# A linear-attention and MoE kernel: a new order for its first block, v loaded amid q, and d_ff columns dealt by fours

## The chip, the cores and the metric

The kernel runs on one core of a Trainium2 chip. The core has a matrix engine (TensorE, PE in the profile, its weight loads listed apart as PEld), a vector engine (VectorE, DVE), an activation engine (ScalarE, ACT), GpSimd (POOL) and a queue engine (SyncE, SP). SP and POOL issue the transfers between device memory and the on-chip memory (SBUF). TensorE writes to PSUM, from where VectorE and ScalarE read. The metric is device time in microseconds (us); lower is better.

## The reference: what is computed

Eight batches of linear attention ("cosformer") feed one two-layer feed-forward block with a quick GELU. Inputs are float32.

```python
# attention: q, k, v are [8 batches, 8 heads, 576 tokens, 64]
theta = pi / 2 * arange(576) / 576
phi(x) = concat([relu(x) * cos(theta), relu(x) * sin(theta)], -1)   # 64 -> 128 features
kv  = einsum('bhsf,bhsd->bhfd', phi(k), v)      # 128 x 64 per head
z   = sum(phi(k), over tokens)                  # 128 per head
num = einsum('bhsf,bhfd->bhsd', phi(q), kv)
den = einsum('bhsf,bhf->bhs', phi(q), z) + 1e-6
x   = (num / den) as [4608 tokens, 512]         # heads side by side
# feed-forward: w_in is [512, 2048], w_out is [2048, 512]
h = x @ w_in
out = (h * sigmoid(1.702 * h)) @ w_out          # [4608, 512]
```

The hidden dimension of 2048 (d_ff) is summed over in the last product, so any reordering of it that is the same for w_in's columns and w_out's rows leaves the output as it is.

## The kernel before

A batch is a *block* of 576 tokens: four chunks of 128 and a tail of 64. The order of instructions on every engine is the order of the program text; no planner moves anything.

**A block's steps.** `trig` makes the features of k or q (relu, times cosine or sine) for one slice j of 64 columns: two instructions, on VectorE or, with `act=True`, on ScalarE. `kv_mm` multiplies features of k by v per head into PSUM (L202), and `kv_evac` copies the result to SBUF as `kvs`. In block 0 a column of ones gives z in a product of its own, before v is there (L364); later blocks carry the ones as a 65th column of v. q's features must be turned so that features lie on partitions: in block 0 TensorE does it (`qturn_pe`, L170) and `qevac` copies the result out of PSUM; later blocks use a transposing transfer on SP's queue. `num_mm` (L215) multiplies turned q by `kvs` for one chunk, giving numerator and denominator. `num_div` on VectorE adds 1e-6, takes the reciprocal and multiplies: three instructions, the last of them writes `xn` (L227). `xturn_mm` (L241) turns `xn` on TensorE and `xturn_evac` (L248, ScalarE) copies it to `xT`. The numerator and the turned x share one PSUM tile `at`, of a pool with two buffers.

**Feed-forward.** d_ff is cut into 16 *groups* of 128 columns, `fc`. `mm1` makes one group for 512 tokens: four matrix products (L264) that load a 128x128 piece of `w_in_sb` as weights, and one activation (L269). `mm1_tail` (L284) does the 64 tail tokens of a block for eight groups: 32 products of only 64 columns with the same weight tiles, 512 of them in the whole kernel. `mm2` (L305) multiplies a chunk of activated tokens by `w_out_sb`, and ScalarE copies the sum out to `ysb` (L309). The PSUM pool `mm` has four buffers.

**The start.** SP's queue loads k in two pieces and then q in two pieces. POOL waits for k's first piece (a one-element copy called `gate`), then issues v in two pieces and w_in's columns in four, the last two behind a second gate on v. TensorE runs products of zeros (`idle`, L317) meanwhile. Then come the ones products, q's first three turns, the K-V products, the fourth turn, the numerators and `start_block(0)`. That function starts the feed-forward chunk by chunk: for each of the four chunks it makes 128-token pieces of groups 0 to 3, with the remaining numerators and x turns between them, and then group 4. Groups 5 to 15 follow as whole groups of 512 tokens.

**Block 1's start.** Here the numerators of chunks 0 to 2 and the x turns of chunks 0 and 1 stand between the last pieces of block 0's `mm2` (L422 to L443), and `start_block(1, opened=True)` leaves them out. Later blocks put their numerators between `mm2` calls and turn x by transfers.

Of the kernel before, what the change touches and what calls it, by code (L numbers as in the profile page):

```python
# [9 lines left out]
F32 = mybir.dt.float32  # L10
# [9 lines left out]
def kernel(  # L20
# [34 lines left out]
    def src_of(src, b, i0=0, i1=NI):  # L55
        return src[b, 2 * i0:2 * i1].rearrange("(i hh) (p j) d -> (hh p) i (j d)", hh=2, j=NS)
# [1 line left out]
    qf = one.tile([128, 2560], F32, name="qf")  # L58
    kf, vf, vb = raw("kf"), raw("vf"), raw("vb", BF16)
    qf0 = qf[:, 0:NI * S].rearrange("p (i e) -> p i e", i=NI)  # L60
    for t, src, cut in ((kf, k, 192), (qf0, q, 256)):
        nc.sync.dma_start(out=t[:, :, 0:cut], in_=src_of(src, 0)[:, :, 0:cut])
        nc.sync.dma_start(out=t[:, :, cut:S], in_=src_of(src, 0)[:, :, cut:S])


    NP = NS + 5
# [36 lines left out]


    win_r = moe_w_in.rearrange("(kc p) f -> p kc f", p=128)
    wout_r = moe_w_out.rearrange("(fc p) d -> p fc d", p=128)

    def load(t, src, b):
        nc.gpsimd.dma_start(out=t, in_=src_of(src, b))
# [7 lines left out]
    def load_win(f0, f1):  # L117
        nc.gpsimd.dma_start(out=w_in_sb[:, :, f0:f1], in_=win_r[:, :, f0:f1])

    def load_wout(g):  # L120
        nc.gpsimd.dma_start(out=w_out_sb[:, ts(g, 4), :], in_=wout_r[:, ts(g, 4), :])

    gate = const.tile([1, 4], F32)
    nc.gpsimd.tensor_copy(gate[0:1, 0:1], kf[0:1, 0, 0:1])
    for i in (0, 2):
        nc.gpsimd.dma_start(out=vb[:, i:i + 2], in_=src_of(v, 0, i, i + 2))
    load_win(0, 512)
    load_win(512, 1024)
    nc.gpsimd.tensor_copy(gate[0:1, 1:2], vb[0:1, 3, 0:1])
    load_win(1024, 1536)  # L130
    load_win(1536, 2048)


    def trig(dst, src, j, act=False):
        i = src[:, :, ts(j, 64)]
        for cs, w in enumerate((cosw, sinw)):
            o = dst[:, j, :, ts(cs, 64)]
            if act:
                nc.scalar.activation(o, i, AF.Relu, scale=w[:, j:j + 1])
            else:  # L140
                nc.vector.tensor_scalar(o, i, 0.0, w[:, j:j + 1], op0=MAX, op1=MUL)  # L141
# [24 lines left out]
    def qturn_pe(c):  # L166
        tp = pmm.tile([128, 2, NI, 128], BF16, name="mm")
        for j in range(2 * c, min(2 * c + 2, NS)):
            for i in range(NI):
                nc.tensor.transpose(tp[:, j % 2, i], qn0[:, j, i, :], ident)  # L170
        tps[c] = tp

    def qevac(c, act=False):
        n = min(2 * c + 2, NS) - 2 * c
        o = qT[:, :, ds(c * 128, n * 64)].rearrange("f h (j p) -> f j h p", j=n)
        i = tps.pop(c)[:, 0:n].rearrange("f j i (hh p) -> f j (i hh) p", hh=2)
        if act:
            nc.scalar.activation(o, i, AF.Copy)
        else:
            nc.vector.tensor_copy(o, i)  # L180
# [16 lines left out]
    def kv_mm(i0, i1, rhs, col, n):  # L197
        for i in range(i0, i1):
            for j in range(NS):
                for hh in range(2):  # L200
                    r = slice(hh * 64, hh * 64 + 64)
                    nc.tensor.matmul(st["kv", i][:, hh, ds(col, n)], kr[r, j, i, :], rhs(r, i, j),  # L202
                                     start=(j == 0), stop=(j == NS - 1))

    def kv_evac(i0, i1):
        o = st["kvs"][:, :, i0:i1, 0:65]
        nc.vector.tensor_copy(o, st["ps", i0].rearrange("p hh (i e) -> p hh i e", e=65))  # L207
# [3 lines left out]
    def num_mm(c):  # L211
        ps = pat.tile([128, 2, 512], F32, name="at")
        for h in range(H):
            i, hh = divmod(h, 2)
            nc.tensor.matmul(ps[:, h // 4, ds((h % 4) * 65, 65)], qT[:, h, ts(c, 128)],  # L215
                             st["kvs"][:, hh, i, 0:65], start=True, stop=True)
        nums[c] = [ps]

    def num_div(c):
        ps = nums[c][0]  # L220
        pv = ps[:, :, 0:260].rearrange("p a (h e) -> p a h e", h=4)
        den = small.tile([128, 2, 4], F32, name="den")
        nc.vector.tensor_scalar(den, pv[:, :, :, 64], 1e-6, None, op0=ADD)  # L223
        inv = small.tile([128, 2, 4], F32, name="inv")
        nc.vector.reciprocal(inv, den)  # L225
        xn = small.tile([128, 2, 4, 64], BF16, name="xn", bufs=4)
        nc.vector.tensor_tensor(xn, pv[:, :, :, 0:64],  # L227
                                inv.unsqueeze(3).to_broadcast([128, 2, 4, 64]), op=MUL)
        nums[c].append(xn)
# [6 lines left out]
    def xturn_mm(c):  # L236
        ps, xn = nums[c]
        xv = xn.rearrange("p a h e -> p (a h e)")
        for kc in range(KC):
            o = ps[:, kc // 2, ds(264 + (kc % 2) * 64, 64)].bitcast(BF16)  # L240
            nc.tensor.transpose(o, xv[:, ts(kc, 128)], ident)  # L241

    def xturn_evac(b, c):
        ps = nums.pop(c)[0]
        n = 128 if c < 4 else 64
        i = ps[:, :, 264:392].bitcast(BF16).rearrange("p a (k t) -> p a k t", k=2)[:, :, :, 0:n]
        o = x[b][:, :, c * 128:c * 128 + n].rearrange("p (a k) t -> p a k t", a=2)
        nc.scalar.activation(o, i, AF.Copy)  # L248
# [11 lines left out]
    def mm1_part(b, fc, t0, t1):  # L260
        if t0 == 0:
            hp[fc] = pmm.tile([128, MT], F32, name="mm")
        for kc in range(KC):
            nc.tensor.matmul(hp[fc][:, t0:t1], w_in_sb[:, kc, ts(fc, 128)], x[b][:, kc, t0:t1],  # L264
                             start=(kc == 0), stop=(kc == KC - 1))

    def gelu(fc):
        g = gpool.tile([128, MT], BF16, name="g")
        nc.scalar.activation(g, hp.pop(fc), AF.Gelu_apprx_sigmoid)  # L269
        gT[fc] = g  # L270

    def mm1(b, fc):
        mm1_part(b, fc, 0, MT)
# [4 lines left out]
    def mm1_tail(b, half):  # L278
        if half == 0 and b % 2 == 0:
            gt[0] = gpool.tile([128, FC, 128], BF16, name="gtail", bufs=2)  # L280
        hps = pmm.tile([128, 8, 64], F32, name="mm")
        for f in range(8):
            for kc in range(KC):
                nc.tensor.matmul(hps[:, f], w_in_sb[:, kc, ts(half * 8 + f, 128)], x[b][:, kc, MT:S],  # L284
                                 start=(kc == 0), stop=(kc == KC - 1))
        nc.scalar.activation(gt[0][:, ts(half, 8), ts(b % 2, 64)], hps, AF.Gelu_apprx_sigmoid)  # L286

# [26 lines left out]
    def idle(n, cols=512):  # L314
        w = pmm.tile([128, 512], F32, name="mm")
        for _ in range(n):
            nc.tensor.matmul(w[:, 0:cols], warm[:, 0:128], warm[:, 0:cols], start=True, stop=True)  # L317
# [4 lines left out]
    def vt_rhs(r, i, j):  # L322
        return vt[r, j, i, 0:65]

    def start_block(b, opened=False):

        if not opened:
            xturn_mm(0)
            xturn_evac(b, 0)
            xturn_mm(1)  # L330
            xturn_evac(b, 1)
            num_mm(2)
            num_div(2)
        for c in range(4):
            for fc in range(4):
                mm1_part(b, fc, c * 128, c * 128 + 128)
            if c == 0:
                num_mm(3)
                num_div(3)
                xturn_mm(2)  # L340
                xturn_evac(b, 2)
            if c == 1:
                num_mm(4)
                num_div(4)
                xturn_mm(3)
                xturn_evac(b, 3)
        for fc in range(4):
            gelu(fc)
        mm1(b, 4)
        xturn_mm(4)  # L350
        xturn_evac(b, 4)


    idle(12)
    idle(100, 64)
    for j in (0, 1):
        trig(kr, kf, j)
    for j in (2, 6, 7, 8):
# [5 lines left out]
    kv_mm(0, NI, lambda r, i, j: ones[r, 0:1], 64, 1)  # L364
    for j in (0, 1):
        trig(qn0, qf0, j)
    qturn_pe(0)
    for j in (2, 3):
        trig(qn0, qf0, j, act=True)
    qturn_pe(1)  # L370
    idle(3)
    for j in (4, 5):
        trig(qn0, qf0, j)
    qturn_pe(2)
    for j in (6, 7):
        trig(qn0, qf0, j, act=True)
    qevac(0)
    trig(qn0, qf0, 8)
    qevac(1, act=True)
    qevac(2, act=True)  # L380
    kv_mm(0, 2, vb_rhs, 0, 64)
    kv_evac(0, 2)
    kv_mm(2, 4, vb_rhs, 0, 64)
    kv_evac(2, 4)
    qturn_pe(3)
    qevac(3, act=True)
    num_mm(0)
    num_div(0)
    num_mm(1)
    num_div(1)  # L390
    qturn_pe(4)
    qevac(4)
    x_open(0)
    start_block(0)


    load(kf, k, 1)
# [5 lines left out]
    load_wout(3)  # L403
    for j in range(NS):
        trig(kr, kf, j)
    for fc in range(5, FC):
        mm1(0, fc)
    mm1_tail(0, 0)
    mm1_tail(0, 1)
# [9 lines left out]
    for g in range(2):  # L419
        for t in range(4):  # L420
            mm2(0, t, 4 * g, 4 * g + 4)
    mm2(0, 0, 8, 12)  # L422
    mm2(0, 1, 8, 12)
    kv_open()
    kv_mm(0, 4, vt_rhs, 0, 65)
    kv_evac(0, 4)
    mm2(0, 2, 8, 12)
    mm2(0, 3, 8, 12)
    num_mm(0)
    num_div(0)  # L430
    num_mm(1)
    num_div(1)
    x_open(1)
    mm2(0, 0, 12, 16)
    mm2(0, 1, 12, 16)
    xturn_mm(0)
    xturn_evac(1, 0)
    mm2(0, 2, 12, 16)
    xturn_mm(1)
    xturn_evac(1, 1)  # L440
    num_mm(2)
    num_div(2)
    mm2(0, 3, 12, 16)  # L443
    start_block(1, opened=True)


    for b in range(1, B):
# [73 lines left out]
```

## Time and profile before

| | |
|---|---|
| median of 3 runs | 296.39 us (295.75 to 305.15) |
| the profiled execution | 295.57 us |
| its span, first to last instruction | 293.9 us |
| PE busy | 283.1 us, 96% of the span |
| VectorE, ScalarE, POOL busy | 42%, 44%, 28% |
| L305 (output products), x509 | 116.0 us |
| L264 (first products), x593 | 113.6 us |
| L284 (tail products), x512 | 16.2 us |
| L202, L215 (K-V, numerators) | 4% and 3% of the chain that ended last |
| transferred | 53.59 MB, mean 182 GB/s |

Times in views run from the span's start. "Busy" counts overlapping products of an engine once. The chain that ended last is followed backwards from the last instruction, from each piece of work to what released it; a piece that reads "issue" is time for which the profile shows no cause. In the groups of instructions, "mean ns of one" is the length of a single instruction from its start to its end; instructions of PE overlap, so their pace is faster than that.

### The profile page before, as it was taken

The page shows a single profiled execution, that of the slowest core. Times are in us where ns is not written, and L with a number is a line of the kernel's source. Part 1 is how long each engine was busy: PE and PEld are TensorE (multiplying, and loading weights), DVE is VectorE, ACT ScalarE, POOL GpSimd, SP SyncE. Part 2 cuts the span into 40 slices and gives each one's busy share as a digit, 9 for nine tenths or more (in the row PEclk, how much of TensorE's full clock was granted, in tenths as well). Part 3 has the DMA queues.
Part 4 walks back from the last instruction along what each step waited for, and adds up shares of the span by engine and source line. Part 5 has one row for each costly group of instructions (what it writes and reads, how often), then busy time and mean ns, then how long its engine had stood idle before and what let it go on. Part 6 is the DMA issues. An engine that isn't in the chain of part 4 may idle for free.

```text
span 293.9 us, 6796 instructions
## 1 busy us (share of the span) xinstructions
PE 283.1 (96%) x2832; PEld 155.7 (53%) x2871; DVE 123.8 (42%) x355; ACT 128.0 (44%) x220; POOL 81.9 (28%) x96
## 2 busy tenths in 40 slices
PE   8879999999999999999999999999999999999993
PEld 4775546746544465446454465446454465445443
DVE  4674513791369125930269115950159304200000
ACT  7847642674115721465114641265114651166121
POOL 6361002635216501470215601290114300100111
PEclk9999999999999999999999999999999999999999
DMA  7999997999999876779249983889258402400112
GB/s 254 239 219 276 351 180 109 326 312 228 323 272 184 240 294 142 156 192 365 71 128 171 221 333 96 151 193 386 85 140 153 93 2 75 115 36 0 38 71 73
DMA packets 64238, 53.59 MB, mean 182 GB/s; under 512 B 49552, under 2 KB 56336, under 8 KB 64208
## 3 DMA queue, kind: packets, MB, share of 16 engines
q0 software_dynamic: 13792, 38.87, 43.3%
q1 hardware_dynamic: 50416, 14.30, 28.4%
q8 instruction: 22, 0.36, 0.5%
q14 instruction: 8, 0.07, 0.1%
HBM read 36.70 MB, written 9.44 MB: 157 GB/s over the span
## 4 chain that ended last, share of the span: by engine, by line
PE 95%; issue 1%; DVE 1%; ACT 1%; ACTq 0%
PE mm L305 42%; PE mm L264 37%; PE mm L284 5%; PE at L202 4%; PE at L215 3%; PE mm L317 3%; PE at L241 1%; DVE xn L227 1%; PE mm L170 1%; ACT g L269 1%; DVE inv L225 0%; DVE den L223 0%; ACT ysb L309 0%; DVE warm L76 0%; ACTq L269 0%
## 5 line engine op out<-in xcount | busy, mean ns | idle before, releaser
L305 PE MATMUL mm<-w_out_sb,g 128*128 128x512 bf16 (+1 forms) x509 | 116.0, 372 | 1.1 <-issue 0.2
L264 PE MATMUL mm<-xT,w_in_sb 128*128 128x512 bf16 (+1 forms) x593 | 113.6, 345 | 0.8
L312 POOL DMA_DIRECT2D out_dram<-ysb x44 | 50.7, 1152 | 169.7 <-ACT ysb L309 162.9
L269 ACT ACTIVATE g<-mm 128x512 bf16<-128x512 f32 x128 | 75.6, 598 | 39.6 <-PE mm L264 39.6
L264 PEld LDWEIGHTS <-w_in_sb 128*128 128x128 bf16 x608 | 53.8, 98 | 55.2
L305 PEld LDWEIGHTS <-g 128*128 128x128 bf16 x528 | 49.0, 98 | 50.2
L309 ACT ACTIVATE ysb<-mm 128x512 f32<-128x512 f32 (+1 forms) x37 | 21.7, 586 | 108.1 <-PE mm L305 101.9
L223 DVE TENSOR_SCALAR den<-at 128x8 f32<-128x8 f32 x40 | 6.6, 166 | 60.6 <-PE at L215 60.6
L227 DVE TENSOR_TENSOR xn<-at,inv 128x512 bf16<-128x512 f32 x40 | 27.7, 691 | 2.4 <-DMA xT<-xn 1.0
L207 DVE CAST kvs<-at 128x520 bf16<-128x520 f32 (+1 forms) x9 | 5.8, 642 | 51.3 <-PE at L202 51.2
L141 DVE TENSOR_SCALAR kr<-kf,cosw 128x256 bf16<-128x256 f32 x68 | 23.8, 350 | 6.9 <-DMA kf<-in_k_dram 6.9
L141 DVE TENSOR_SCALAR kr<-kf,sinw 128x256 bf16<-128x256 f32 x68 | 23.1, 340 | 0.0
L215 PEld LDWEIGHTS <-qT 128*128 128x128 bf16 x320 | 14.5, 97 | 7.3
L154 DVE TENSOR_SCALAR qn<-qf,cosw 128x512 bf16<-128x512 f32 (+1 forms) x33 | 15.8, 478 | 3.9 <-DMA qf<-in_q_dram 3.9
L284 PEld LDWEIGHTS <-w_in_sb 128*128 128x128 bf16 x512 | 16.0, 98 | 1.9
L284 PE MATMUL mm<-xT,w_in_sb 128*128 128x64 bf16 x512 | 16.2, 193 | 0.1
L215 PE MATMUL at<-kvs,qT 128*128 128x65 bf16 x320 | 15.9, 193 | 0.0
L154 DVE TENSOR_SCALAR qn<-qf,sinw 128x512 bf16<-128x512 f32 (+1 forms) x33 | 15.8, 479 | 0.0
L305 PE MATMUL mm<-w_out_sb,gtail 128*128 128x512 bf16 x60 | 13.6, 379 | 0.2
L202 PEld LDWEIGHTS <-kr 64*128 64x128 bf16 x648 | 10.1, 94 | 4.3 <-issue 3.7
L286 ACT ACTIVATE gtail<-mm 128x512 bf16<-128x512 f32 x16 | 9.6, 597 | 5.1 <-PE mm L284 5.1
L317 PE MATMUL mm<-warm 128*128 128x64 bf16 (+1 forms) x114 | 8.7, 240 | 1.3 <-DVE warm L76 1.3
(54 smaller groups left out, 112.0 us busy)
## 6 DMA issues: line engine op xcount, KB each, us to landing
kf<-in_k_dram POOLq DMA_DIRECT2D x7, 1152.0 KB, 9.1
vf<-in_v_dram POOLq DMA_DIRECT2D x7, 1152.0 KB, 11.8
qf<-in_q_dram POOLq DMA_DIRECT2D x7, 1024.0 KB, 7.4
out_dram<-ysb POOLq DMA_DIRECT2D x27, 256.0 KB, 2.8
out_dram<-ysb POOLq DMA_DIRECT2D x17, 128.0 KB, 7.2
w_in_sb<-in_moe_w_in_dram POOLq DMA_DIRECT2D x4, 512.0 KB, 9.7
w_out_sb<-in_moe_w_out_dram POOLq DMA_DIRECT2D x4, 512.0 KB, 18.0
qf<-in_q_dram POOLq DMA_DIRECT2D x7, 128.0 KB, 7.4
```

The lines of the kernel that those rows point to most:

```text
L141: nc.vector.tensor_scalar(o, i, 0.0, w[:, j:j + 1], op0=MAX, op1=MUL)
L154: nc.vector.tensor_scalar(o, i, 0.0, sc, op0=MAX, op1=MUL)
L202: nc.tensor.matmul(st["kv", i][:, hh, ds(col, n)], kr[r, j, i, :], rhs(r, i, j), start=(j == 0), stop=(j == NS - 1))
L215: nc.tensor.matmul(ps[:, h // 4, ds((h % 4) * 65, 65)], qT[:, h, ts(c, 128)], st["kvs"][:, hh, i, 0:65], start=True, stop=True)
L227: nc.vector.tensor_tensor(xn, pv[:, :, :, 0:64], inv.unsqueeze(3).to_broadcast([128, 2, 4, 64]), op=MUL)
L264: nc.tensor.matmul(hp[fc][:, t0:t1], w_in_sb[:, kc, ts(fc, 128)], x[b][:, kc, t0:t1], start=(kc == 0), stop=(kc == KC - 1))
L269: nc.scalar.activation(g, hp.pop(fc), AF.Gelu_apprx_sigmoid)
L284: nc.tensor.matmul(hps[:, f], w_in_sb[:, kc, ts(half * 8 + f, 128)], x[b][:, kc, MT:S], start=(kc == 0), stop=(kc == KC - 1))
L305: nc.tensor.matmul(yp[t, c0][:, c0:c1], w, w_out_sb[:, fc, c0:c1], start=(fc == 0), stop=(fc == FC - 1))
L309: nc.scalar.activation(ysb[:, c0:c1], yp[t, c0][:, c0:c1], AF.Identity)
L312: eng.dma_start(out=dst[:, c0:c1], in_=ysb[p0:p0 + n, c0:c1])
L317: nc.tensor.matmul(w[:, 0:cols], warm[:, 0:128], warm[:, 0:cols], start=True, stop=True)
```

## The change

Three things are changed together.

1. *Loads.* SP's queue loads k and q's first 256 columns of each row. v follows behind POOL's gate as before, then q's other columns on POOL's queue, then w_in: two transfers of 512 columns and, behind the gate on v, one of 1024 in place of two of 512.
2. *Order at the start of blocks 0 and 1.* Block 0 writes its start out by hand: K-V stands between the second and third turn of q, and the feed-forward begins with eight groups instead of five. Chunks 0 and 1 of groups 0 to 3 are made in pieces of 128 tokens, groups 4 to 7 in halves of 256 tokens (`half_part`); the activation then takes 256 tokens of two groups at once (`half_gelu`). The warm-up products are 111 of 64 columns, 16 of 128 and 6 of 512, in place of 12 of 512 and 100 of 64; three more of 512 between turns go. Block 1's start is no longer spread through block 0's output products: its K-V products stand ahead of groups 8 to 11 of `mm2`, two numerators stand between groups 12 to 15, and the rest is in `start_block(1)` behind them.
3. *d_ff dealt by fours.* Group fc = 4g + c now holds columns 512g + 4f + c, for f from 0 to 127. w_out's rows lie accordingly, so each partition of a w_out transfer reads four neighbouring rows, 8 KB, instead of four rows of 2 KB that lie apart. w_in is still loaded with neighbouring columns side by side; so a weight tile is now every fourth of 512 columns (`wcol`), in all products that load w_in.

The core of the diff:

```diff
-    for t, src, cut in ((kf, k, 192), (qf0, q, 256)):
-        nc.sync.dma_start(out=t[:, :, 0:cut], in_=src_of(src, 0)[:, :, 0:cut])
-        nc.sync.dma_start(out=t[:, :, cut:S], in_=src_of(src, 0)[:, :, cut:S])
+    nc.sync.dma_start(out=kf[:, :, 0:192], in_=src_of(k, 0)[:, :, 0:192])
+    nc.sync.dma_start(out=kf[:, :, 192:S], in_=src_of(k, 0)[:, :, 192:S])
+    nc.sync.dma_start(out=qf0[:, :, 0:256], in_=src_of(q, 0)[:, :, 0:256])
...
-    wout_r = moe_w_out.rearrange("(fc p) d -> p fc d", p=128)
+    wout_r = moe_w_out.rearrange("(g p c) d -> g p c d", p=128, c=4)
...
-        nc.gpsimd.dma_start(out=w_out_sb[:, ts(g, 4), :], in_=wout_r[:, ts(g, 4), :])
+        nc.gpsimd.dma_start(out=w_out_sb[:, ts(g, 4), :], in_=wout_r[g])
+    def wcol(kc, fc):
+        g, c = divmod(fc, 4)
+        return w_in_sb[:, kc, ts(g, 512)].rearrange("p (f c) -> p f c", c=4)[:, :, c]
...
+    nc.gpsimd.dma_start(out=qf0[:, :, 256:S], in_=src_of(q, 0)[:, :, 256:S])
     load_win(0, 512)
     load_win(512, 1024)
-    nc.gpsimd.tensor_copy(gate[0:1, 1:2], vb[0:1, 3, 0:1])
-    load_win(1024, 1536)
-    load_win(1536, 2048)
+    nc.gpsimd.tensor_copy(gate[0:1, 1:2], vb[0:1, 2, 0:1])
+    load_win(1024, 2048)
...
-            nc.tensor.matmul(hp[fc][:, t0:t1], w_in_sb[:, kc, ts(fc, 128)], x[b][:, kc, t0:t1],
+            nc.tensor.matmul(hp[fc][:, t0:t1], wcol(kc, fc), x[b][:, kc, t0:t1],
...
+    def half_part(fc, c0, c1):
+        pr, u, h = fc // 2, fc % 2, c0 // 2
+        if u == 0 and c0 % 2 == 0:
+            hb[pr, h] = pmm.tile([128, 2, 256], F32, name="mm")
+        t0, t1 = c0 * 128, c1 * 128
+        for kc in range(KC):
+            nc.tensor.matmul(hb[pr, h][:, u, t0 - h * 256:t1 - h * 256], wcol(kc, fc), x[0][:, kc, t0:t1],
+                             start=(kc == 0), stop=(kc == KC - 1))
+    def half_gelu(pr, h):
+        if h == 0:
+            gp[pr] = gpool.tile([128, 2, MT], BF16, name="gpair", bufs=4)
+            gT[2 * pr], gT[2 * pr + 1] = gp[pr][:, 0], gp[pr][:, 1]
+        nc.scalar.activation(gp[pr][:, :, ts(h, 256)], hb.pop((pr, h)), AF.Gelu_apprx_sigmoid)
...
-    idle(12)
-    idle(100, 64)
+    idle(111, 64)
+    idle(16, 128)
+    idle(6)
...
     for j in (2, 3):
         trig(qn0, qf0, j, act=True)
+    qturn_pe(0)
     qevac(0)
     kv_mm(0, 2, vb_rhs, 0, 64)
     kv_evac(0, 2)
+    qturn_pe(1)
+    qevac(1, act=True)
     kv_mm(2, 4, vb_rhs, 0, 64)
     kv_evac(2, 4)
     num_mm(0)
     num_div(0)
     num_mm(1)
     num_div(1)
+    for j in (4, 5):
+        trig(qn0, qf0, j, act=True)
+    x_open(0)
+    xturn_mm(0)
+    xturn_evac(0, 0)
+    qturn_pe(2)
+    qevac(2)
+    xturn_mm(1)
+    xturn_evac(0, 1)
+    trig(qn0, qf0, 6)
+    trig(qn0, qf0, 7, act=True)
+    half_part(0, 0, 1)
+    half_part(1, 0, 1)
+    num_mm(2)
+    num_div(2)
+    half_part(2, 0, 1)
+    half_part(3, 0, 1)
+    trig(qn0, qf0, 8)
+    for fc in range(4):
+        half_part(fc, 1, 2)
+    half_gelu(0, 0)
+    half_gelu(1, 0)
+    qturn_pe(3)
+    qevac(3)
+    xturn_mm(2)
+    xturn_evac(0, 2)
+    half_part(4, 0, 2)
+    half_part(5, 0, 2)
+    half_gelu(2, 0)
+    num_mm(3)
+    num_div(3)
+    half_part(6, 0, 2)
+    half_part(7, 0, 2)
+    half_gelu(3, 0)
+    qturn_pe(4)
+    qevac(4)
+    xturn_mm(3)
+    xturn_evac(0, 3)
+    for c in (2, 3):
+        for fc in range(4):
+            half_part(fc, c, c + 1)
+    half_gelu(0, 1)
+    half_gelu(1, 1)
+    num_mm(4)
+    num_div(4)
+    for fc in (4, 5, 6, 7):
+        half_part(fc, 2, 4)
+    half_gelu(2, 1)
+    half_gelu(3, 1)
+    xturn_mm(4)
+    xturn_evac(0, 4)
...
-    for fc in range(5, FC):
+    for fc in range(8, FC):
         mm1(0, fc)
...
-    mm2(0, 0, 8, 12)
-    mm2(0, 1, 8, 12)
     kv_open()
     kv_mm(0, 4, vt_rhs, 0, 65)
     kv_evac(0, 4)
-    mm2(0, 2, 8, 12)
-    mm2(0, 3, 8, 12)
+    for t in range(4):
+        mm2(0, t, 8, 12)
+    x_open(1)
+    mm2(0, 0, 12, 16)
+    mm2(0, 1, 12, 16)
     num_mm(0)
     num_div(0)
     num_mm(1)
     num_div(1)
-    x_open(1)
-    mm2(0, 0, 12, 16)
-    mm2(0, 1, 12, 16)
-    xturn_mm(0)
-    xturn_evac(1, 0)
     mm2(0, 2, 12, 16)
-    xturn_mm(1)
-    xturn_evac(1, 1)
-    num_mm(2)
-    num_div(2)
     mm2(0, 3, 12, 16)
-    start_block(1, opened=True)
+    start_block(1)
```

## The prediction

> **What bounds the kernel now.** I read the page first: engines, then the chain that ended last.
>
> ```profile
> PE 283.1 (96%) x2832; PEld 155.7 (53%) x2871; DVE 123.8 (42%) x355; ACT 128.0 (44%) x220; POOL 81.9 (28%) x96
> PE 95%; issue 1%; DVE 1%; ACT 1%; ACTq 0%
> ```
>
> TensorE (PE) is the path almost everywhere. This change makes no multiplication fewer, so it can only win idle time of PE; the question is where that lies. The chain in order of time, from 9 to 25 us, has most of it:
>
> ```profile
> 12.33 0.28 PE at L202 x12
> 12.61 1.07 issue
> 13.68 1.07 PE at L202 x60
> ...
> 15.30 0.26 PE at L215 x8
> ...
> 16.02 0.69 DVE xn L227
> ...
> 17.06 0.70 DVE xn L227
> 17.76 0.05 issue
> 17.80 0.40 PE at L241 x4
> ...
> 18.92 0.69 DVE xn L227
> ...
> 19.87 0.38 PE at L241 x4
> ...
> 24.66 0.43 PE mm L264 x2
> ```
>
> Columns: start, length, what. The reader should see VectorE's division (L227) between PE's pieces, and a gap of 1.07 us inside the K-V product that no engine explains ("issue"). The DMA view for 11 to 12 us has one 0.02 MB packet on the instruction queue, and none from 0 to 11, so I read the gap as PE waiting for its program. From 9.25 (first ones product) to 24.66 (d_ff group 5) are 15.41 us. The PE work in it, at the pace of this chain: ones 0.98, 36 q transposes 2.0, K-V 1.3, five numerators at 0.24, five x transposes at 0.22, 64 pieces of 128 tokens at 0.056 (32 in 1.79) and one group of 512 at 0.86: 11.0. So 4.4 us are idle or filler, and **4.4 us is the ceiling** of what a new start can win.
>
> The chain from 44 to 59 us, block 1's start, has hardly any idle time: three numerators and two x transposes are already spread through the output products.
>
> ```profile
> 47.69 0.48 PE at L215 x16
> 48.17 1.73 PE mm L305 x8
> 49.90 0.22 PE at L241 x4
> 50.12 0.86 PE mm L305 x4
> 50.98 0.22 PE at L241 x4
> ```
>
> **Part 1, v before q's second half.** The gate on POOL waits until 12.15 for v:
>
> ```profile
> 12.15 0.17 POOL L129 CAST gate<-vb 1x1 f32<-1x1 bf16 x1 [4.75 <-DMA vb<-in_v_dram]
> ```
>
> Until then k, q and v, 3.54 MB of float32, have moved; between 4 and 8 us the stretches show 383 to 395 GB/s. v now passes 0.655 MB of q: 1.6 us, so v lands at about 10.5, and q's second half at about 12.2 (it landed near 9.7). That DMA goes from SP's queue to POOL's, one issue of about 0.8 us (POOL's issues here take 0.75 to 0.96), ahead of w_in; POOL is idle from 7.4 to 12.15, so it is free. The bytes ahead of w_in are unchanged; its landings from the starts and landing times of its four issues (8.2 to 11.1 us) and POOL's waits: about 15.1, 17.8, 20.6, 23.3. Merging the last two saves one issue and makes groups 8 to 11 wait for 23.3 instead of 20.6.
>
> **Part 2, the new order in block 0**, stepped through with durations from the timeline. Warm-up: twelve products of 512 columns run at 0.43 us until about 5.9, later ones at 0.216, so PE's pace doubles there. Products of 64 run 41 to the us afterwards (24 ns), so I take 49 before: some 95 of 111 by 5.9, the rest 0.4, then 16 at 0.056 and 6 at 0.216 = 2.2; PE is free at 8.5 and waits for the last k feature on ScalarE (8.22 + 0.49 = 8.7). Then ones to 9.7, first q turn 10.2, K-V of two head pairs (36 at 0.018) 10.9, second turn 11.4, K-V 12.0, its evacuation (0.43) 12.5. The first numerator starts at 12.5 instead of 15.1. xn follows 1.63 us after it (15.08 to 16.71) and the second 1.04 later: 14.15 and 15.2. ScalarE does q slices 4 and 5 from 12.4 to 14.0 beside it, in the shadow of the division. x chunk 0 is out at 15.25, just behind w_in's first quarter at 15.1; the first w_in product starts at 15.5 instead of 18.28. From there work for eight groups instead of four fills the divisions: groups 0-3 in 128s (3.58), 4-7 in 256s (32 at 0.109, half of 0.216), three numerators, three x turns, two q turns and a bit: 8.8 us, and 0.6 us of waits (xn of chunk 3 comes at 20.6, PE is there at 20.45; ScalarE's queue of half activations delays x chunk 2 to 19.4, which PE needs only at 20.9). Group 8 starts at 24.9; now it starts at 24.66 + 12 x 0.216 = 27.25. That is **-2.35 us**. The cover is w_in: groups 4-7 need 17.8 and start near 18.3, groups 8 on need 23.3; if these slip by x, PE waits x less 0.5 and 1.6.
>
> The unknown here is the program gap. PE reaches the same number of instructions again inside the first K-V product, so it may come again: +1.07, or 0. I take 1.07, since that is what the row has: **-1.3** (ends: -2.35, and no gain, if the data waits return).
>
> The half activations cost nothing extra: eight of 512 columns as before (0.60 each).
>
> **Part 3, block 1's start.** All five numerators but two, and all x turns, now stand behind the last output product. Call T the start of the first numerator. PE: two numerators (0.49), two output pieces (1.73): T+2.2, x turn 0 to T+2.45. The second xn comes at T+2.8 (now: 47.31 to 50.13), so PE waits 0.35. On ScalarE, x chunk 0's copy is queued behind two output copies of 0.6 (T+2.4 to T+3.6, counting its own); the third numerator needs the PSUM buffer that this copy frees (two buffers of that pool): 0.55 idle. Then x turn 2 waits for xn 2, 1.6 us after its numerator, with 0.9 + 0.25 of work beside it: 0.4. Sum 1.3, against about 0.3 in the present chain: **+1.0** (0.3 to 1.5). K-V for block 1 moves 1.7 us ahead; v's copies end at 40.2, and it starts near 41, so it stays covered.
>
> **Part 4, d_ff by fours.** w_out's pieces of 8 KB change transfers that land before use (issues from 14.5 on, first use at 35.86, 14 to 20 us to landing): 0. But every w_in load into PE now reads each fourth element, for which no row exists. Where it would show is the tail product:
>
> ```profile
> L284 PE MATMUL mm<-xT,w_in_sb 128*128 128x64 bf16 x512 | 16.2, 193 | 0.1
> L284 PEld LDWEIGHTS <-w_in_sb 128*128 128x128 bf16 x512 | 16.0, 98 | 1.9
> ...
> 104.56 1.87 PE mm L284 x64
> ```
>
> 64 load-and-multiply pairs in 1.87 us are 29.2 ns each: a load that keeps up costs nothing. Groups of 512 tokens have 216 ns to hide one. Ends: 0, and loads one after another at the 98 ns of a single one: 512 x 68.8 = +35.2, plus 128 pieces of 128 tokens x 42 = +5.4. A gain is excluded: PE already runs at the pace of the shorter products after it. In between, a load twice as long: the ones products load 72 half-height tiles in 0.98 us, 27 ns for two halves, so 54 ns, 512 x 25 = +12.9. I take 0: nearest to the rows in which all weight loads, of eight tiles and two heights, take the same 94 to 103 ns.
>
> The Trainium skill, "TensorE: Matmul & The Clock Gate", section "Weight-path perf modes — Fast Weight Load (FWL) and DoubleRow", bears on this twice. It keeps the fast load for column steps from -1,023 to 1,024 elements, which would make the cost 0. It also says that the fast load reads 32 bits, two bf16, at a time, which speaks against the change, because columns four apart are never neighbours. By its "LDWEIGHTS" section a load without the fast mode takes 128 / 1.2 = 107 ns, an estimate that makes the sum some 40 us longer.
>
> **Sum** against the profiled execution (295.57, of which 293.9 are span; the median of the three runs, 296.39, is 0.8 above it): 295.57 - 1.3 + 1.0 + 0 = **295.3 us**. A measurement here can tell about 2%, or 6 us, from no change.
>
> **Rivals.**
> - *The dealt columns slow the weight load* (ends on the other side). Place: L284's 512 pairs. For it: no strided load has been seen and the pairs are at the pace of the multiplication. Against: the equal rows above. Price: 295.3 + 12.9 = 308; at 98 ns 336. It decides from 29.2 + 6/512 = 41 ns a pair. Chance 0.24.
> - *The start is won whole:* no program gap (-2.35) and block 1 at +0.3: 293.5. Chance 0.15.
> - *Nothing is won at the start:* v shares the engines with q after all, or w_in's first quarters come 1.3 us later; block 1 still pays 1.0: 296.6. Chance 0.16. This is the case in which the change doesn't do what it says.
> - *The forecast:* 0.45, its own range 294.3 to 296.3.
>
> Over 2% faster is out of reach by the ceiling of 4.4 us: 0.01. Slower by over 2% is nearly the first rival alone: 0.24; within: 0.75. The range holds the three cases near 295 with a us of spread, and the doubled load of the first rival: 293.0 to 308.5.
>
> **What to look for after.** v's gate at 10.5; first numerator at 12.5 (13.6 with the gap); first w_in product at 15.5 to 16.5; group 8 at 25 to 26; in block 1's start a gap of half a us before the first w_in product; and each L284 stretch still 1.87 us per 64. Stretches of 3.5 us would make the prediction wrong by the first rival, a wait for w_in in groups 4 to 8 by the third.

## The result and the profile after

The changed kernel takes **306.68 us** (median of 6 runs, 305.92 to 308.92) against 296.1 before (median of 6): a ratio of 1.0371, with a 95% interval from 1.0333 to 1.0408. It is slower. Ratios compare runs of the faster of two states in which a kernel's runs fall, while medians and ranges take in all runs, such as the 305.15 us of the kernel before. The changed kernel's profiled execution took 305.92 us, 304.1 of it span: 10.2 us more than the span before.

The page of the changed kernel, engines and the chain that ended last (lines of code have moved: L305 is now L329, L264 is L270, L284 is L308, and L287 is the new `half_part`):

```profile
PE 289.4 (95%) x2905; PEld 170.6 (56%) x2905; DVE 124.5 (41%) x355; ACT 127.3 (42%) x220; POOL 83.4 (27%) x96
PE 92%; DMA 4%; DVE 2%; issue 0%; ACT 0%; POOL 0%; ACTq 0%
```

A transfer has 4% of the chain now, where none had a share before. The chain from 8 to 28 us says which one (start, length, what):

```profile
9.16 0.99 PE at L208 x72
10.15 0.57 PE mm L176 x8
...
11.94 11.39 DMA w_in_sb<-in_moe_w_in_dram
...
23.47 0.91 PE mm L287 x7
24.38 0.44 PE at L221 x8
24.82 2.37 PE mm L287 x24
```

Read against the chain before, the beginning went as foreseen: the gap of 1.07 us in the K-V product is gone and the first w_in product starts at 16.0 instead of 18.28. But it is alone. PE does one product of the first group, then stands still until the *last* w_in transfer has landed at 23.3. PE's timeline (start, length, what, idle time before it and what ended it) and the waits from 8 to 30 us (engine, line, waited for: us, times, longest) show it:

```profile
16.01 0.24 PE L287 MATMUL mm<-xT,w_in_sb 128*128 128x128 bf16 x1
23.47 0.91 PE L287 MATMUL mm<-xT,w_in_sb 128*128 128x128 bf16 x7 [7.21 <-DMA w_in_sb<-in_moe_w_in_dram]
```

```profile
PE mm L287 <- DMA w_in_sb<-in_moe_w_in_dram: 7.2, 1, 7.2
```

Two stretches of 1 us, one in the wait and one behind it, show a second price (length, busy us of PE, PEld, DVE, ACT, POOL, then granted clock, DMA share, GB/s):

```profile
18.00:19.00 1.00, 0.00 (x0) 0.00 (x0) 0.00 (x0) 0.00 (x0) 0.00 (x0) 0.50 1.14 215
...
24.00:25.00 1.00, 1.00 (x16) 1.00 (x15) 0.15 (x1) 0.00 (x0) 0.00 (x0) 0.50 1.06 333
```

The granted clock is half from 17 to past 26 us. It was 0.81 in the us from 16 to 17, so it fell when the wait had hardly begun, behind two us in which PE was busy for 0.52 and 0.44 (13 to 15 us) and one of 0.91. It was still half when the transfer landed, so the work after the wait runs at 0.099 us a product of 128 tokens (24 in 2.37) instead of 0.056. The groups 0 to 3 of d_ff, which the waiting product needs, had landed at about 16; nothing in the computation needs columns 1024 to 2047 before group 8. The program's own list of instructions shows the wait where it is made. The three w_in transfers carry the marks 3, 4 and 5:

```
651 L287 Ldweights w_in_sb [waits DMASW3_49]
652 L287 Matmult mm<-xT,w_in_sb 128x128 [waits Activation_49]
653 L287 Ldweights w_in_sb [waits DMASW5_49,DMASW4_49]
```

In the kernel before the four transfers are waited for one by one, each ahead of the first group that reads it.

The first load waits for mark 3 alone, and the layout says why. In each partition the buffer holds four stretches of 2048 columns, one for each 128 rows of w_in. The first load reads every fourth column from 0 to 508 of the first stretch; they lie ahead of everything that the transfers of marks 4 and 5 write. The second load reads the same columns of the second stretch. These lie between the first and the last column that each of those transfers writes, without being among them. So the waits fit a comparison by first and last element alone; how the program comes to them is not shown.

The groups of instructions for the tail products have the second loss, a single load 118 ns instead of 98:

```profile
L308 PEld LDWEIGHTS <-w_in_sb 128*128 128x128 bf16 x512 | 18.4, 118 | 1.8
L308 PE MATMUL mm<-xT,w_in_sb 128*128 128x64 bf16 x512 | 18.5, 198 | 0.0
```

In the chain 64 pairs take 2.13 us instead of 1.87:

```profile
113.39 2.13 PE mm L308 x64
```

And PE's timeline has the third, at block 1's start: the third numerator waits for ScalarE's copy, as the prediction had it.

```profile
60.41 0.40 PE L221 MATMUL at<-kvs,qT 128*128 128x65 bf16 x8 [0.48 <-ACT xT L254]
```

The difference of 10.2 us, place by place: block 0's tail products start at 41.51 instead of 34.00 (+7.5); group 5 of block 1 starts at 66.67 instead of 58.15 (+8.5; 0.26 of the new microsecond is the slower tail, 0.75 block 1's start); and seven more groups of 64 tail pairs at 0.26 each make 1.8.

### The profile page after: what moved, and what is told of

The parts are those of the page before. It is cut to its first block, busy times and chain, and to the rows that moved or that the text cites. A ratio compares the mean times of both kernels' runs of the same rounds, so it can differ in the third digit from the quotient of the medians.

```text
span 304.1 us, 6896 instructions
## 1 busy us (share of the span) xinstructions
PE 289.4 (95%) x2905; PEld 170.6 (56%) x2905; DVE 124.5 (41%) x355; ACT 127.3 (42%) x220; POOL 83.4 (27%) x96
## 4 chain that ended last, share of the span: by engine, by line
PE 92%; DMA 4%; DVE 2%; issue 0%; ACT 0%; POOL 0%; ACTq 0%
PE mm L329 40%; PE mm L270 34%; PE mm L308 6%; DMA w_in_sb<-in_moe_w_in_dram 4%; PE at L208 3%; PE at L221 3%; PE mm L341 3%; PE mm L287 3%; DVE xn L233 1%; PE at L247 1%; PE mm L176 0%; DVE inv L231 0%; DVE qT L186 0%; DVE den L229 0%; ACT xT L254 0%
## 5 line engine op out<-in xcount | busy, mean ns | idle before, releaser
L329 PE MATMUL mm<-w_out_sb,g 128*128 128x512 bf16 (+1 forms) x496 | 110.0, 372 | 0.0
L270 PE MATMUL mm<-xT,w_in_sb 128*128 128x512 bf16 (+1 forms) x528 | 106.8, 360 | 0.0
L336 POOL DMA_DIRECT2D out_dram<-ysb x44 | 46.8, 1064 | 173.5 <-ACT ysb L333 169.9
L275 ACT ACTIVATE g<-mm 128x512 bf16<-128x512 f32 x120 | 71.2, 598 | 38.6 <-PE mm L270 38.6
L270 PEld LDWEIGHTS <-w_in_sb 128*128 128x128 bf16 x528 | 55.7, 114 | 46.2
L329 PEld LDWEIGHTS <-g 128*128 128x128 bf16 x496 | 46.1, 98 | 47.1
L308 PEld LDWEIGHTS <-w_in_sb 128*128 128x128 bf16 x512 | 18.4, 118 | 1.8
L308 PE MATMUL mm<-xT,w_in_sb 128*128 128x64 bf16 x512 | 18.5, 198 | 0.0
L112 POOL DMA_DIRECT2D qf<-in_q_dram x7 | 12.4, 1778 | 16.3 <-issue 13.0
L287 PE MATMUL mm<-xT,w_in_sb 128*128 128x128 bf16 (+1 forms) x96 | 9.7, 264 | 7.2 <-DMA w_in_sb<-in_moe_w_in_dram 7.2
L329 PE MATMUL mm<-w_out_sb,gtail 128*128 128x512 bf16 x64 | 14.5, 379 | 0.0
```

The costliest lines, as they stand in the source:

```text
L112: nc.gpsimd.dma_start(out=qf[:, 0:2048].rearrange("p (h e) -> p h e", h=H), in_=q[b, :, 0:512, :].rearrange("h (p c) d -> p h (c d)", c=4))
L270: nc.tensor.matmul(hp[fc][:, t0:t1], wcol(kc, fc), x[b][:, kc, t0:t1], start=(kc == 0), stop=(kc == KC - 1))
L287: nc.tensor.matmul(hb[pr, h][:, u, t0 - h * 256:t1 - h * 256], wcol(kc, fc), x[0][:, kc, t0:t1], start=(kc == 0), stop=(kc == KC - 1))
L308: nc.tensor.matmul(hps[:, f], wcol(kc, half * 8 + f), x[b][:, kc, MT:S], start=(kc == 0), stop=(kc == KC - 1))
L329: nc.tensor.matmul(yp[t, c0][:, c0:c1], w, w_out_sb[:, fc, c0:c1], start=(fc == 0), stop=(fc == FC - 1))
L336: eng.dma_start(out=dst[:, c0:c1], in_=ysb[p0:p0 + n, c0:c1])
```

## The experiments

Theory **needless wait**: a strided tile of a buffer that is filled by strided transfers is taken to overlap with transfers that don't touch it, so the second weight load waits for the whole of w_in. Rivals: **late data** (the first quarters really land late behind v and q) and **slow loads** (the strided loads cost the ten microseconds themselves). The first four kernels ran together, beside 296.0 us for the kernel before.

### w_in held by quarters

```diff
-    w_in_sb = one.tile([128, KC, d_ff], BF16, name="w_in_sb")
+    w_in_sb = one.tile([128, 4, KC, 512], BF16, name="w_in_sb")
...
+        for g in range(f0 // 512, f1 // 512):
+            nc.gpsimd.dma_start(out=w_in_sb[:, g], in_=win_r[:, :, ts(g, 512)])
...
+        return w_in_sb[:, g, kc].rearrange("p (f c) -> p f c", c=4)[:, :, c]
```

> The changed kernel with w_in held quarter by quarter in SBUF (each transfer fills one unbroken stretch of a partition; columns still dealt by fours; the last 1024 columns come as two transfers of 512 again). Theory 'needless wait': the second weight load of block 0 waits for all of w_in only because a strided tile and a strided transfer of the same buffer are taken to overlap. Then the wait of 7.2 us goes, and the half clock after it; group 8 starts near 25.5 instead of 34.6; the tail stretches stay at 2.13 us per 64. Time 306.7 - 9.1 = about 297.5. Rival 'late data' (the first quarters really land late behind v and q): the gap stays, 306.7. Rival 'slow loads' (the strided loads themselves cost the ten us): no change, 306.7.

299.11 us, ratio 1.012 (1.0079 to 1.0161). The gap is gone. From the chain:

```profile
15.77 0.64 PE mm L288 x8
16.40 0.24 PE at L222 x8
16.64 1.35 PE mm L288 x24
...
25.40 6.91 PE mm L271 x32
32.31 2.13 PE mm L309 x64
```

Group 8 starts at 25.4 and the tails keep 2.13: both as the needless wait has it, and 7.6 us come back. The two rivals fall as the cause of the bulk. But 297.5 was expected and 299.1 came: PE waits twice later on, 1.06 us for block 2's turned q at 83 us and 0.27 us at its K-V, and 0.52 us with no cause shown at 140 us. The runs further down take up such waits.

### d_ff in order, the rest as changed

```diff
-        return w_in_sb[:, kc, ts(g, 512)].rearrange("p (f c) -> p f c", c=4)[:, :, c]
+        return w_in_sb[:, kc, ts(fc, 128)]
```

(w_out's rows go back likewise.)

> The changed kernel with d_ff in order (neighbouring columns as weights, w_out in 2 KB pieces); new order of blocks 0 and 1 and the new loads stay. Theory 'needless wait': wait gone, since unbroken tiles are told apart, and strided loads gone too: tail stretches 1.87 us, 2.1 us less than the run with quarters: about 295.4. Rival 'late data': gap stays, tails quicker: 304.6. Rival 'slow loads': all of the loss goes here, 296, and nothing of it in the run with quarters.

302.03 us, ratio 1.0206 (1.0162 to 1.0249). The first gap is gone here too (group 8 at 25.5) and the tails are at 1.87. The merged w_in transfer is still there, so it wasn't the split of that transfer into two that helped the run with quarters. But 295.4 was expected by the theory, and PE's timeline has new stalls:

```profile
67.32 1.26 PE L208 MATMUL at<-vt,kr 64*128 64x65 bf16 x72 [1.18 <-DVE vt L168]
...
94.22 15.89 PE L270 MATMUL mm<-xT,w_in_sb 128*128 128x512 bf16 x60 [4.32 <-DMA xT<-xn]
```

Block 2's K-V waits for v's copies, and block 2's first products wait 4.3 us for a turning transfer of x, and the granted clock is 0.50 from 94 to 99 us. PE had been 0.8 us ahead of the kernel before at block 1's group 5 (57.34 against 58.15).

### The kernel before with dealt columns, one buffer and by quarters

The first of the two deals the columns as in the change's third part, in the kernel before; the second also holds w_in by quarters.

> The kernel before with the columns dealt by fours and nothing else changed. Theory 'needless wait': the second weight load waits for the last quarter of w_in here too, from about 18.4 to 23.3; about 5 us, some 1.5 us of half clock after it, and 2.1 us of slower tails: 296.1 + 8.6 = 304.7. Rival 'late data' (v amid q is to blame): no gap, 298.2. Rival 'slow loads': 306.

> The kernel before with the columns dealt by fours and w_in held quarter by quarter. This leaves the price of the strided load alone. Theory 'needless wait': no gap, tails at 2.13 instead of 1.87 us per 64, 8 stretches: 296.1 + 2.1 = 298.2. Rival 'slow loads': near 306. Were the pieces of 8 KB worth anything, it would be under 298.

303.91 us (ratio 1.0268, 1.0252 to 1.0283) and 297.67 us (1.004, 1.0024 to 1.0056). The first waits, in an order and with loads that were not touched; its chain:

```profile
13.09 10.30 DMA w_in_sb<-in_moe_w_in_dram
...
23.52 1.76 PE mm L268 x15
```

The last w_in transfer is one of four of equal size here, so neither the merged transfer nor v amid q makes the wait; dealing the columns in one buffer does. The second has no such gap. It costs 1.7 us by the medians and 1.2 by the ratio, 2.1 by the sum (eight groups of tails at 0.26 more each, as their 2.13 has it). The pieces of 8 KB win nothing that shows. In its kept trace PE also waits 0.54 us for block 2's turned q, at 85 us, so a wait of this kind isn't the new order's alone.

### Block 0's start and block 1's start, each alone

The first kernel has d_ff in order, the changed block 0 and loads, and block 1's start of before. The second is the kernel before with block 1's changed start. (Their edits are those parts of the change.)

> The changed kernel with d_ff in order (w_out in 2 KB pieces) and with block 1's start as in the kernel before; block 0's new order and the new loads stay. Theory 'transfers set the pace': block 0 ends about 1.7 us earlier and block 1's groups start near 56.6 instead of 58.3, but block 2's K-V cannot start before about 67, when k's features and v's copies from the transfers of block 2 are ready; so it waits 1.5 to 2 us there and the turning transfers of x may be late again near 90 us: 296 to 302, not under 295. Rival 'block 1's new start made the stalls': no stall, 295.96 - 1.7 = 294.3.

> The kernel before with block 1's start as in the changed kernel and nothing else. Both theories: group 5 of block 1 starts 0.75 us later (a gap of half a us before the third numerator). 'Transfers set the pace': K-V of block 2 then waits for nothing: 296.7. Rival 'block 1's new start made the stalls': waits near 67 and 90 us as with columns in order: 300 to 302.

299.31 us (ratio 1.014, 1.0048 to 1.0232) and 296.68 us (1.0013, 0.9974 to 1.0051). Block 1's start by itself costs 0.4 us by the ratio, at most 1.5 by its interval, and has the gap of 0.48 us; its kept trace has no stall at 67 or 90 us. Block 0's new order, free of the needless wait and of strided loads, is still slower than the old one. The chain that leads to block 2's K-V, from 47 to 69 us, shows one thing it runs into:

```profile
47.40 2.87 DMA qT<-qn
...
51.05 0.87 POOL qf L112
51.91 7.46 DMA qf<-in_q_dram
...
59.41 3.50 DVE qn L160 x9
62.91 2.47 DVE kr L147 x10
...
67.64 1.28 DVE vt L168
...
68.96 1.26 PE at L208 x72
```

Nothing of PE stands in it from 37 us on: the turning transfers of block 1's q, POOL's gate on them, block 2's q, VectorE's features in order, v's copies. The chain of the kernel before runs through PE there. This one run also had v land 1.4 us later than the run with columns in order (7.2 us after its issue instead of 5.8), PE half idle from 14 to 16 us, and a granted clock of 0.50 from 17 to 20; group 8 started only at 28.0. PE reached block 1's group 5 at 58.85 us, behind the 58.15 of the kernel before, and still waited 1.31 us at block 2's K-V: here it is the features and copies that are late, and not PE that is early.

### An earlier gate, and a filled start

```diff
-    nc.gpsimd.tensor_copy(gate[0:1, 2:3], qT[0:1, 7, S - 1:S])
+    nc.gpsimd.tensor_copy(gate[0:1, 2:3], qT[0:1, 7, 511:512])
```

```diff
     qevac(0)
+    idle(1)
     kv_mm(0, 2, vb_rhs, 0, 64)
...
     num_div(1)
+    idle(4)
```

> Block 0's new order, block 1's old start, columns in order (299.3 us in its first form), and POOL's gate ahead of block 2's loads now waits for the fourth turned chunk of block 1's q instead of the fifth (one element read from column 511 instead of 575). Theory 'transfers set the pace': q of block 2 lands about 2 us earlier, VectorE's features and v's copies with it, and K-V of block 2 no longer waits 1.3 us: about 2 us less than 299.3, 297; if the clock also stays up at the start, 294.5. Rival 'the start's loss is only the clock': K-V's wait goes on and the time stays at 299.

> The kernel before with the same earlier gate and nothing else: the control. In the kernel before K-V of block 2 waits for nothing, so an earlier q of block 2 is worth nothing: 296, within 0.5. If it gains, the gain of the run before it isn't from the wait at K-V; if it loses, the earlier loads slow the last turn of block 1's q.

> The run with the earlier gate, and five products of zeros (512 columns each) put into the start: one ahead of the first K-V product, four behind the second numerator, where PE is idle for about 1 us. If the half clock from 16 to 20 us comes of those idle stretches, PE's rate is whole there, group 8 starts near 25.5 instead of 28, and the time is about 294.3. If the clock falls all the same, 297.

> Block 0's new order, block 1's old start, columns in order, the old gate, and the five products of zeros. The clock stays whole at the start, so PE is 1.7 us ahead at block 1's groups; by 'transfers set the pace' it then waits for v's copies of block 2 until about 67 us, and nothing of the 1.7 us is left: 296, or more if the turning transfers of x come late as in the run with columns in order (302.0). By the rival, 'the start's loss is only the clock', 294.3.

The gate: 298.54 us (1.0069, 1.0028 to 1.011) with the new block 0, and 295.86 (0.9996, 0.9962 to 1.0031) in the kernel before. It hardly opened earlier: at 50.2 and 48.5 us, against 50.4 and 49.3 without the edit. So it was no test of the theory, and brought nothing that can be told from run to run. In the kept trace of the kernel before with this gate PE waits 2.11 us for block 2's turned q, at 85.7 us; without it, for nothing. In the kept traces of the two filled kernels, both of runs of 300 us and more, the granted clock is 1.00 throughout the start. That the fillers did it is not shown. Without them it was also 1.00 with columns in order, where PE was busy for 0.12 of the us from 13 to 14; and with the earlier gate alone it was 0.50 from 12 to 21 us, behind four us in which PE was busy for 0.63 to 1.00. Group 8 started at about 26.5 us with the earlier gate, where 25.5 had been expected, and at 27.2 without it. With the earlier gate the time was 297.55 us (1.0011, 0.9965 to 1.0057), from 294.15 to 306.33 in its eleven runs; without it, 295.24 to 303.93 in four, too wide for a verdict. Seven of the eleven runs spread over 3.8 us (294.15 to 297.92) and four lie above, where 15 of the 26 runs of the kernel before lie within one microsecond.

### Block 2's loads left out

```diff
-    load_q(2)
-    load(kf, k, 2)
-    load(vf, v, 2)
```

> As the filled start with the old gate, but the three loads of block 2 (q, k, v, 3.5 MB) are left out: block 2 computes from block 1's q, k and v. Theory 'transfers set the pace': nothing is left to wait for at block 2's K-V near 67 us and less to collide with the turning transfers of x, so the start's 1.7 us stay: about 1.7 us under the kernel before with the same loads left out, some 294. Rival 'the new order is no quicker in itself': level with it or slower.

> The kernel before with the same three loads of block 2 left out (block 2 computes from block 1's q, k and v). PE waits for none of them in the kernel before, so about 296, at most 0.5 less. It is what the run with the new start and fewer loads is compared with.

294.26 us (ratio to the kernel before 0.9914, 0.9877 to 0.9951) with the new start, its six runs from 293.14 to 295.15; 294.81 us (0.995, 0.9925 to 0.9975) with the old one. The scatter is smaller, and the kept trace has no wait at K-V or at x's turn. The start's lead now lasts. Block 3's K-V in the chain, new start and then old:

```profile
100.79 1.19 PE at L208 x72
```

```profile
101.95 1.19 PE at L202 x72
```

The new start is 1.16 us ahead here. It was as far ahead behind block 1's K-V (44.40 against 45.56), and it is 1.1 ahead in the spans (291.7 and 292.8), but only 0.55 in the medians. The runs of the two kernels overlap (294.42 to 295.49 with the old start), and so do the intervals of the ratios. So the traces say that the new order is quicker in itself, by most of what the sum gave, and the times point the same way without being clear of the noise. With block 2's loads in place the filled start was level with the kernel before (1.0011 with the earlier gate). That points at these transfers as what takes the lead back; it isn't shown, since both differences lie within the noise.

The old start gained 1.5 us from the omission by the ratio of 0.995, where I had said 0.5 at most. The kept traces don't put this gain with the loads. Without them PE is 0.45 us ahead behind block 1's K-V (45.56 against 46.01), before POOL's gate, behind which these loads stand, opens at 49.4. It is 0.45 ahead at the last copy to `ysb` too (289.00 against 289.45); the rest of the 1.1 us between the spans (292.8 and 293.9) falls behind that copy.

### The step of a strided load

The kernel before with columns dealt by eights and by sixteens, w_in held in stretches to suit.

> The kernel before with the columns dealt by eights: a weight tile is every eighth of 1024 columns, and each half of w_in lies in an unbroken stretch. Only the price of the strided load is looked at. If a step of 16 bytes costs twice the row reads of a step of 8: tail stretches well over 2.13 us per 64, up to 3.5; if it is only the step that costs, 2.13 again. A single load took 98 ns with neighbouring columns and 118 dealt by fours.

> The kernel before with the columns dealt by sixteens over all of w_in (a step of 32 bytes). Block 0's first product really needs all four transfers now, so it waits to 23.3 as the dealt kernels with one buffer did: a start about 5 us later by a true need. Tail stretches: as dealt by eights if the price saturates once each column lies in its own 16 bytes, longer if it goes on growing.

311.86 and 318.64 us, one run each. The stretch of 64 tail pairs in the chains, dealt by four (by quarters), eight and sixteen:

```profile
105.89 2.13 PE mm L289 x64
```

```profile
109.30 3.83 PE mm L289 x64
```

```profile
115.31 3.96 PE mm L289 x64
```

With neighbouring columns it is 1.87. A pair takes 29.2, 33.3, 59.8 and 61.9 ns with the columns 2, 8, 16 and 32 bytes apart: nearly free to 8, twice at 16, and no more after that. Dealt by sixteens the first product waits 4.8 us for all of w_in, by a true need.

## Why the prediction was wrong

The forecast was 295.3 us, and the step that failed is in part 2: "The cover is w_in: groups 4-7 need 17.8 and start near 18.3, groups 8 on need 23.3". I gave every product the landing of the columns it reads. The program gives the second product the landing of all columns, because of part 4, and I never asked of the dealt tile what it would wait for, only what it would cost to load. Where I had -1.3 us by block 0's end, +7.5 were measured: 7.2 of waiting, and the work behind it at half the clock. Taking the wait away gives 7.6 us back in the changed kernel, and adding it to the kernel before costs 6.2 (303.91 against 297.67).

By its steps:

- *v at 10.5 us, first numerator at 12.5, first w_in product at 15.5.* The gate on v reads 11.8, the first numerators stand at 12.5 to 13.1, the first product at 16.0. Right within half a us to 1.3 us. The program gap, which I had charged with 1.07 us, did not come in the changed kernel.
- *Group 8 at 24.9 to 26 without further waits.* 25.4 and 25.5 in the two runs without the needless wait: the sum of the start was right. But it was not the end of the account. I took the start's gain for the kernel's, and never asked what PE would meet when it came early. With columns in order it met block 2's transfers, which a PE that comes sooner doesn't hasten: 1.18 us at K-V and 4.32 at x's turn. Of the 1.3 us, 1.1 were seen in two spans, with those loads left out, and 0.55 in the medians.
- *Block 1 +1.0.* 0.75 in the changed kernel, the gap of half a us at the third numerator where I had put it. Alone in the kernel before, 0.4 us by the ratio of 1.0013, and not told apart from nothing.
- *Dealt columns at 0, with 12.9 for a load twice as long.* The place was right and the size wrong, in both figures: 4.1 ns a pair, 2.1 us. The price of 12.9 (25 ns a pair) belongs to a step of 16 bytes, where 30.6 ns a pair were measured.
- *The first rival*, slower by dealt columns through L284, had the sign and the culprit, but its mechanism pays for 2.1 of the 10.2 us. The 308 us it gave are near the measured 306.68 by chance.

The Trainium skill bears on the load twice. "TensorE: Matmul & The Clock Gate", section "Weight-path perf modes — Fast Weight Load (FWL) and DoubleRow", says that a fast load reads two bf16 at a time: with columns four apart there are no such neighbours, and the pair took 33.3 ns all the same, so the cost I had drawn from it, some 40 us, is not there. "SBUF — State Buffer", section "Door 1: The DMA port swizzle", has reads go by lines of 16 bytes, and at least two hits in a line for full rate; it gives a free step of eight bf16. Columns four apart lie two to such a line, columns eight apart one. The jump from 33.3 to 59.8 ns between four and eight agrees with the two hits and not with the eight.

## What to carry to other kernels

A new layout has a second price beside its access: what the program will make it wait for. Before you cost a strided view, list the waits of the first instructions that use it; hold each transfer's data in a stretch of its own; in both kernels tried here the false ones went with that. And a gain at the start is one only if what PE meets later has slack too: follow the chain of transfers of the next two blocks before you count it.

## What else the runs showed of the hardware

- PE's clock can fall at the start without a full stop, and need not fall with one nearly full. In the run with block 0's new order alone PE was about half busy from 14 to 16 us (0.49 and 0.53 in two stretches of 1 us) and had a granted clock of 0.50 from 17 to 20. With the earlier gate added it had 0.50 from 12 to 21, behind stretches with PE busy for 0.63 to 1.00. With columns in order it kept 1.00 behind a stretch of 0.12. Of the five kept traces with the new start and no fillers it fell in three, in the changed kernel's before the wait was 1 us old; in the three with five products of zeros it didn't. What decides it is not shown.
- A weight load's step costs in one jump: 29.2, 33.3, 59.8, 61.9 ns for a load and a product of 64 columns at 2, 8, 16, 32 bytes.
- With 3.5 MB of loads left out that PE was not seen to wait for, the kernel before kept its pace: in the kept traces it is 0.45 us ahead before these loads are issued and 0.45 at the last copy.
